# First batch's causal masks added in PSUM by TensorE, half of its q and k loaded as f16 by software DMA, and the hand-written order of all steps replaced

## The chip, the cores and the metric

The kernel runs on one core of one Trainium2 chip. The metric is the device time of one execution in microseconds (us). The engines are named as the profile names them: PE is TensorE's matmuls and PEld its weight loads, DVE is VectorE, ACT is ScalarE, POOL is GpSimd, and SP is SyncE, which here only issues DMAs. POOL issues the software DMAs (queue q0 of the profile), SP and ACT the hardware ones (q1).

## What is computed

For 8 batches of 8 heads, 576 tokens and 64 features a head, with 16 beacon keys ahead of the ordinary ones, attention is followed by a mixer over tokens and a two-layer perceptron:

```python
k_all = np.concatenate([beacon_k, k], axis=2)
v_all = np.concatenate([beacon_v, v], axis=2)
scores = scale * np.matmul(q, k_all.transpose(0, 1, 3, 2))
causal[:, Nb:] = np.triu(np.ones((S, S), dtype=bool), k=1)
scores = np.where(causal, -1000000000.0, scores)
a = softmax(scores)                # exp(scores - max) / sum
x = matmul(a, v_all)               # heads side by side: 8 x 576 x 512
u = x + (x^T @ U @ V)^T            # mixer of rank 32 over the tokens
out = u + relu(u @ w_ch1) @ w_ch2  # 512 -> 2048 -> 512
```

Inputs and outputs are f32. The kernel works in f16 with f32 sums in PSUM.

## The kernel before

**Units of work.** A "pair" is two heads of one batch, 32 pairs in all: pairs 0 to 3 are batch 0, pairs 4 to 7 batch 1, and so on. For a pair, q and k come in from HBM (`main_load` for the last 512 tokens, `head_load` for the first 64, `beacon_load` for the beacon keys). A step G (`regroup`, L251) copies the main part into a pair tile `pr`; for batch 0, whose loads arrive as f32 in `stm` and `sth`, a step H (`first_heads`, L742) also casts the head part into `hd`. A step T transposes q or k on PE (L261, L263) and copies it out of PSUM into `qT` or `kT` by DVE (L264, L265) or ACT (L109); from batch 3 on steps R let a transposing DMA do this. In the script GqV2 reads: regroup q of pair 2 by VectorE; A stands for ScalarE.

**Scores.** `score_units` (L298) makes a pair's scores in four visits, Sa to Sd, of widths 496, 464, 496 and 208 (`groups`). A visit multiplies for both heads, which sit in partitions 0 to 63 and 64 to 127 (L316, 64 rows each), and ACT takes the exponential from PSUM into one of four buffers `expt` (L321), two for each pair. Steps M (`mask_head`, L302), two a pair, then cap the masked entries on DVE: one `min` against `bigmask` over four diagonal blocks of 128 (L304) and one over the last block of 80 (L306). The caps are 65504 where a key is allowed and 0 where it isn't. Steps A (`av_unit`, L325) multiply with v (L331) and divide by the row sums on DVE (L339, L340).

**Mixer and perceptron.** X steps (`mix_units`) make `uT`: Xb.0 is `qtp` (L371), Xb.1 and Xb.2 are the `ups` products (L390, L397) and their copies by DVE and ACT. The perceptron runs in nine blocks of 512 tokens: g steps (L529, 16 a block, each four matmuls of 512 columns, ReLU by ACT and DVE), p steps (sums of operands on DVE), P steps (second layer, L620), U steps (transposing DMAs). The last three blocks make the first layer by F steps (L566).

**Order.** Nothing is scheduled at run time. `SCRIPT` (L855 on) is a list of steps, and each engine gets its instructions in the order of that list. An engine executes in order, so an instruction that waits holds all that stand behind it on its engine. Two kinds of steps do no needed work: I1 is one filler matmul of 512 columns (`keep_warm`, L239), and an ending such as ":3" on a visit puts three fillers ahead of it. A lower-case k, q, b, v or w issues a group of DMAs on POOL; for instance q1A loads q of batch 1's first four heads. Each DMA waits for the one eight places before it in its queue, whose semaphore it reuses.

**Loads of batch 0.** `load_first` (L691) puts pair 0's q on ACT's queue with the beacon keys; pair 0's k and pairs 1 to 3 are 14 DMAs on SP, all f32. v comes by POOL in halves of four heads, v0A and v0B. POOL's next loads are q1A and k1A, then w12, a quarter of the first weight matrix.

Of the kernel before, what the change touches and what calls it, by code (L numbers as in the profile page):

```python
# [9 lines left out]
F16 = mybir.dt.float16  # L10
F32 = mybir.dt.float32
# [6 lines left out]
P = 128  # L18
# [9 lines left out]
def kernel(  # L28
# [86 lines left out]
    bigmask = const.tile([P, 4, P], F16, name="bigmask", tag="bigmask")  # L115

# [181 lines left out]
    def score_units(c, qT, kT, ex):  # L298
# [11 lines left out]
        def visit(g, idle=0):  # L310
            ps = [pst([P, 512], F32, name=f"sps{i}") for i in range(2)]
            keep_warm(ps[0], idle)
            for ch, qa, w, o in groups[g]:
                for i in range(2):
                    hp = slice(D * i, D * i + D)
                    nc.tensor.matmul(  # L316
                        ps[i][:, ds(o, w)], kT[hp, c, ds(P * ch, P)], qT[hp, c, ds(qa, w)],
                        start=True, stop=True,
                    )
            for i in range(2):  # L320
                nc.scalar.activation(  # L321
                    out=ex[i][:, ds(PAD + SLOT * g, gw[g])], in_=ps[i][:, 0 : gw[g]], func=AF.Exp, scale=scale
                )
# [367 lines left out]
    def load_first():  # L691

        main = gtp.tile([P, 2, H, 4 * D], F32, name="stm", tag="gT")
        head = gtp.tile([P, 2, H, D], F32, name="sth", tag="gT")
        raw["head"] = head
        hd = [loads.tile([P, H, D], F16, name=f"hd{i}", tag=f"hd{i}") for i in range(2)]
        Ls[0] = hd, [main[:, i, :, :] for i in range(2)]

        def kload(hs):
            main_load(nc.sync, k[0], main[:, 0, hs, :], hs)  # L700
            head_load(nc.sync, k[0], head[:, 0, hs, :], hs, Nb)

        def qload(eng, hs):
            main_load(eng, q[0], main[:, 1, hs, :], hs)
            head_load(eng, q[0], head[:, 1, hs, :], hs, 0)

        qload(nc.scalar, SETS[0])
        kload(SETS[0])
        beacon_load(nc.scalar, beacon_k[0], head[:, 0, :, :], ALLH)

        nc.scalar.activation(out=warm, in_=ones, func=AF.Exp)
        for hs in SETS[1:]:
            kload(hs)
            qload(nc.sync, hs)
# [19 lines left out]
    def group(p, i, copy):  # L734
# [3 lines left out]
        regroup(Ls[b], c, i, copy, prs[p])  # L738
        if b == 0 and not any(t[0] == "H" and t[1] == "kq"[i] and t[3:] == str(p) for t in SCRIPT.split()):
            first_heads(c, i, copy)  # L740
# [21 lines left out]
    def scores_of(p):  # L762
        b, c = divmod(p, NH2)
        if p not in scs:
            scs[p] = score_units(c, qT_of(b), kTs[b % 2], ex_of(p))
# [25 lines left out]
    def step(t):  # L791
# [7 lines left out]
        elif name in "kqbv":  # L799
# [5 lines left out]
            elif name == "b":  # L805
                beacon_load(nc.gpsimd, beacon_k[b], L_of(b)[0][0], ALLH)
# [49 lines left out]
        HqA0 I1 GkA0 I1 I1 I1 GqA0 I1 I1 HkV0 u I1 I1 I1 GkV1 I1 B I1 I1 I1 TqA0 TkA0 I1 TkV1 I1 s v0A  # L856
        Sd0 Sb0 Sa0:3 I1 GqV1 TqV1 GkV2 Sc0 I1 GqV2 v0B I1 I1 Sc1 Sb1 I1 M0.0 Sd1 M0.1 TqV2 TkV2 I1 A0.0
        I1 GqV3 Sa1:2 A0.1 M1.0 Sd2 I1 GkV3 q1A M1.1 Sc2 TqA3 Sb2 I1 k1A Sa2:1 TkV3 I1 M2.0 I1 A1.0 I1
        A1.1 Sd3 Sa3:1 w12 I1 Sb3 cV M2.1 GqV4 A2.1 b1 k1B TqV4 GkA5 Sc3 I1 GkV4 I1 M3.0 q1B eA GqV5
        TkV4 I1 GkV7 TkA5 I1 w13 A2.0 Sd4 M3.1 I1 TqV5 A3.0 GkA6 b2 w10 I1 A3.1 k2 Sa4 I1 Sd5 GqV6 GqV7  # L860
        TkA7 X0.0 X0.1 Sa5:0 X0.2 Sb4 TqV7 TqV6 Sc5 TkA6 v1A g0.9 Sc4 M4.1 Sb5 M5.1 U0.0 U0.2 g0.13
        GkV11 g0.1 M5.0 g0.10 g0.0 GkV8 g0.14 q2 g0.3 g0.11 GkA9 A5.0 A5.1 Sb7 I1 w11 TkV8 GqV8 GqV9 Sa7
        g0.2 M4.0 GqV11 Sd7 Sc7 TkV11 TkA9 g0.8 A4.1 M7.0 TqA9 A4.0 p00.0 p00.1 Sb6 v1B Sa6:0 g0.12
        p00.2 TqV11 M7.1 Sc6 g0.4 Sd6 g0.15 M6.0 GkA10 w20 U0.1 M6.1 TqV8 g0.6 A7.1 A7.0 Sd9 Sc9 w21
        A6.1 g0.7 A6.0 Sd8 g0.5 Sc8 Sa8 GqV10 X1.0 v2 b3 p01.0 p01.2 X1.1 P02.0 p01.1 X1.2 W0 P01.0 Sb8
        W4 W5 W1 Sb9 Sa9 W2 U1.1 W6 P01.1 TkA10 P02.1 M8.1 M9.0 TqA10 W7 b4 M8.0 U0.3 P05.0 P05.1 q3
        P06.0 P06.1 M9.1 A8.1 A9.0 A8.0 Sa10 P03.0 P03.1 k3 g1.15 A9.1 q4 Sa11 Sd10 g1.5 g1.1 Sb10 Sc10
        g1.3 g1.2 GkV13 GqA12 M10.0 GkA12 W3 P07.0 M10.1 P07.1 GqA13 Sb11 Sd11 GqA14 Sc11 M11.1 g1.9
        M11.0 GkA14 g1.12 A10.0 g1.7 g1.10 g1.0 R12 R13 R14 g1.6 TkV12 TqV12 TkV13 P04.0 GqA16 A11.1
        g1.8 U1.0 U1.3 TqA13 GkA15 P04.1 g1.14 A11.0 k4 A10.1 Sa13 Sd12 g1.11 p10.0 g1.4 GqA17 g1.13  # L870
        Sa12 Sb12 Sc12 p11.0 GqV15 X2.0 M12.0 P11.0 GkA17 P11.1 U1.2 X2.1 GkV16 p11.1 R15 P12.0 P12.1
        R16 P16.0 TqV14 Sd13 Sb13 M12.1 p10.1 p10.2 Sc13 P16.1 b5 U2.2 M13.0 TkA14 v3 A12.1 q5 A12.0 R17
        GkA19 P15.0 P15.1 p11.2 Sa14 Sd14 Sc14 x12 P17.0 TkV15 M13.1 P13.0 U2.3 A13.0 Sb14 Z16 M14.0
        P17.1 P13.1 GqA19 GqA18 TkV16 TqA16 A13.1 g2.13 g2.10 TqV17 TqV15 M14.1 v4 g2.4 Sa15 k5 Sc15
        TkA17 P14.0 A14.0 P14.1 A14.1 Sd16 GqV20 Sb15 Sd15 M15.1 GkV18 g2.0 x14 Sc16 M15.0 g2.7 g2.5
        g2.2 A15.0 A15.1 x13 Sd17 Sb17 g2.9 U2.0 X3.0 b6 Sa16 X2.2 g2.3 x15 Sa17 Sb16 R18 R19 Z18 GkV20
        M16.1 Sc17 M17.1 M17.0 g2.1 g2.6 g2.12 M16.0 g2.8 g2.15 A17.0 U2.1 TqA19 GqA21 TqA18 X3.1 A16.1
        A17.1 g2.14 A16.0 X3.2 g2.11 p21.0 P21.0 P21.1 GqA23 GkA21 q6 TkA18 p20.0 P22.0 P22.1 TkA19 R20
        p21.1 p20.1 Sc18 Sb18 P26.0 P26.1 R21 Sc19 Sd18 Sa19 p21.2 P25.0 P25.1 GkV22 p20.2 I1 Sd19 Sa18
        M18.0 U3.0 Sb19 M19.0 P27.0 M18.1 M19.1 P23.0 GqV24 GqA22 TqV20 P27.1 x16 P23.1 g3.11 TqA21  # L880
        GkV23 TkV20 TkA21 R22 b7 A19.1 g3.7 A19.0 R23 g3.13 g3.8 g3.5 Sa21 Sb21 Sc21 P24.0 P24.1 A18.1
        A18.0 Sb20 U3.3 Sd21 Sa20 M21.1 M21.0 g3.3 g3.2 Sc20 Sd20 X4.0 g3.4 M20.0 k6 GkV24 M20.1 g3.15
        GqA26 N5 v5 TkV22 g3.12 A21.0 U3.1 A20.0 g3.10 N1 GkA26 g3.1 x17 q7 g3.0 A20.1 TqV22 TqA23 TkV23
        g3.6 g3.14 g3.9 p30.0 p30.2 A21.1 Sc23 GkV25 p31.0 Sb23 GqV25 Sa23 R24 p30.1 x18 P31.0 P31.1
        GkV27 P32.0 P32.1 TkA24 p31.1 Sc22 p31.2 U3.2 k7 Sd22 v6 Sa22 P36.0 P36.1 Sb22 x19 M22.1 Sd23
        M23.0 P35.0 R25 R26 M22.0 P35.1 X4.1 P37.0 P37.1 X4.2 GqV27 TqA24 TqA25 P33.0 U4.1 P33.1 TkA25
        P34.0 R27 g4.0 GqV28 A22.1 TkV26 GkA28 R28 M23.1 g4.11 GqV29 g4.2 g4.6 TqV26 A23.0 g4.10 A23.1
        Sd25 Sc25 A22.0 g4.4 GkV29 R29 Sb25 GkV30 Sa25 M25.0 Sd24 TqV27 P34.1 TkA27 g4.3 U4.3 TkV28
        M25.1 g4.15 g4.13 g4.9 Sc24 Sa24 x21 Sb24 M24.0 U4.2 X5.0 A25.0 M24.1 g4.8 g4.12 U4.0 GqV31 x22
        g4.1 p40.0 p40.1 GqA30 A25.1 g4.7 Sa27 Sb27 A24.1 g4.14 A24.0 g4.5 p41.0 GkV31 Sc27 x23 Sc26  # L890
        p41.2 p41.1 Sd26 P41.0 P41.1 Sa26 Sd27 M27.1 Sb26 P45.0 p40.2 P42.0 P42.1 P45.1 TkA29 x20 X5.1
        U5.3 A27.1 R30 TqV29 M27.0 P46.0 P46.1 P43.0 P43.1 g5.13 A27.0 M26.0 M26.1 Sd29 g5.11 X5.2 g5.4
        U5.1 TqV28 P47.0 g5.2 A26.1 TkA30 x27 P47.1 A26.0 N0 Sb29 Sc29 R31 N4 g5.6 N2 Sb28 Sa29 g5.0 x24
        P44.0 g5.15 TqA30 M29.1 P44.1 x25 Sd28 Sa28 v7 Sc28 M28.1 M28.0 A29.1 g5.7 g5.14 TkV31 g5.1 g5.5
        M29.0 A28.0 g5.3 N3 A28.1 Sb30 TqV31 Sa30 g5.10 A29.0 U5.0 g5.12 g5.9 x29 g5.8 N6 p51.0 p51.2
        X6.0 p50.0 Sb31 Sd30 p50.1 x26 p51.1 Sc31 P51.0 P51.1 Sd31 p50.2 Sc30 M30.0 M30.1 Sa31 M31.0 x28
        U5.2 P52.0 M31.1 P56.0 X6.1 P55.0 A31.1 V6.0 U6.1 V6.2 P56.1 A31.0 x31 P52.1 A30.1 A30.0 V6.1
        x30 P57.0 P55.1 P57.1 X6.2 X7.0 N7 P53.0 P53.1 U6.2 F61.3 X7.2 P54.0 P54.1 F62.3 F61.2 X7.1
        F66.3 F62.2 F61.0 F65.0 V6.3 F65.3 V7.0 F62.0 U7.2 F66.2 F65.1 F67.3 F63.3 F61.1 F66.0 F62.1
        F63.0 F64.3 F66.1 F65.2 F67.2 F71.3 F67.0 F75.0 F67.1 F63.1 U7.0 F71.0 V7.1 F64.0 U7.3 F63.2  # L900
        p61.0 V8.0 P61.0 V7.3 F64.2 F64.1 F76.0 F76.3 U7.1 p61.1 U6.3 p60.0 p60.1 p60.2 U6.0 P61.1 P62.0
        P62.1 P65.0 p61.2 P65.1 guard V7.2 P66.0 P66.1 P63.0 P63.1 F75.3 F72.0 F72.3 F75.2 F77.0 F73.0
        P67.0 P67.1 F73.3 F71.1 F71.2 F72.1 F72.2 F76.1 F76.2 F75.1 V8.2 V8.1 P64.0 P64.1 F77.1 F77.2
# [127 lines left out]
```

## Time and profile before

| what | us |
|---|---|
| median of 3 runs | 338.99 (338.74 to 339.47) |
| the profiled execution | 339.2 |
| its span | 337.5 |
| outside the span | 1.7 |
| PE busy | 327.8 |
| ACT busy | 228.0 |
| DVE busy | 264.8 |
| first matmul, a filler | starts at 1.59 |
| first exponential | starts at 8.89 |
| first mixer matmul (X0.0) | starts at 30.06 |
| last matmuls of the output | about 332.9 |

Times in the trace count from the start of the span. In the views, "idle" or "waits" name what ended the wait. A busy PE is not a PE at its peak, since fillers count as busy, and so does the time in which matmuls drain. A row of the timeline may merge neighbours on an engine ("x14"); the end that it shows is that of the last one's pipeline, so where PE rows follow each other, the distance of their starts is what the work took.

### The profile page before, as it was taken

How to read it: one execution, taken by the hardware profiler on the slowest of the kernel's cores; microseconds unless marked ns; L12 is line 12 of the kernel's file. 1: busy time of each engine (PE TensorE's matmuls, PEld its weight loads, DVE VectorE, ACT ScalarE, POOL GpSimd, SP SyncE). 2: the span in 40 equal slices, each digit the busy share in tenths (PEclk: the TensorE clock that was granted, in tenths of full speed). 3: DMA queues.
4: the chain of work that ended last, by engine and by line, in shares of the span. 5: the costliest groups of instructions: out<-in, count | busy, mean ns of one | idle time of the engine just before them, and what ended most of it. 6: DMA issues, size and time to landing. Idle time of an engine off the chain costs nothing.

```text
span 337.5 us, 8954 instructions
## 1 busy us (share of the span) xinstructions
PE 327.8 (97%) x3527; PEld 228.0 (68%) x3527; DVE 264.8 (78%) x690; ACT 228.0 (68%) x494; POOL 99.3 (29%) x129
## 2 busy tenths in 40 slices
PE   7989999999999999999999999999999999999994
PEld 3446466765678655766577547765688888888883
DVE  2888588985778757875888868886999999896882
ACT  4897898749778889878785799267912842644500
POOL 9765662340621602450024410000002503303300
PEclk9999999999999999999999999999999999999999
DMA  9999999999999999999979997554545501203042
GB/s 178 221 196 196 153 167 195 98 168 175 164 180 176 169 188 150 124 136 187 189 109 145 172 183 96 83 114 100 51 62 161 93 2 63 80 0 95 3 113 98
DMA packets 136145, 44.17 MB, mean 131 GB/s; under 512 B 108417, under 2 KB 131969, under 8 KB 136097
## 3 DMA queue, kind: packets, MB, share of 16 engines
q0 software_dynamic: 69008, 17.54, 61.3%
q1 hardware_dynamic: 66496, 25.66, 42.0%
q8 instruction: 29, 0.48, 0.6%
q10 hardware_dynamic: 592, 0.34, 0.3%
q14 instruction: 20, 0.16, 0.2%
HBM read 37.63 MB, written 9.44 MB: 139 GB/s over the span
## 4 chain that ended last, share of the span: by engine, by line
PE 75%; DVE 16%; DMA 3%; issue 3%; ACT 2%; SPq 0%; DVEq 0%; ACTq 0%
PE gps L529 23%; PE cpY L620 15%; PE po L331 8%; PE sps L316 8%; PE cpD L620 7%; PE cpA L620 3%; PE fpY L566 3%; DMA stm<-in_q_dram 3%; DVE gT L581 3%; DVE sT L601 2%; DVE ob L645 2%; DVE uT L404 2%; PE fpD L566 2%; PE tps L263 1%; ACT expt L321 1%
## 5 line engine op out<-in xcount | busy, mean ns | idle before, releaser
L321 ACT ACTIVATE expt<-sps 128x496 f16<-128x496 f32 (+2 forms) x256 | 111.6, 538 | 15.8 <-PE sps L316 14.3
L529 PE MATMUL gps<-uT,w 128*128 128x512 f16 x384 | 91.8, 379 | 0.0
L620 PEld LDWEIGHTS <-gT 128*128 128x128 f16 x576 | 54.6, 98 | 10.5 <-issue 2.2
L529 PEld LDWEIGHTS <-w 128*128 128x128 f16 x384 | 34.3, 98 | 37.4 <-issue 2.5
L587 POOL TENSOR_SCALAR gT<-gT 128x512 f16<-128x512 f16 x12 | 17.8, 1495 | 105.6 <-DVE gT L581 89.0
L620 PEld LDWEIGHTS <-sT 128*128 128x128 f16 x432 | 41.0, 98 | 7.8 <-issue 2.0
L331 PEld LDWEIGHTS <-expt 128*128 128x128 f16 (+1 forms) x960 | 35.5, 98 | 9.2 <-DVE expt L304 1.3
L203 POOL DMA_DIRECT2D vs<-in_v_dram x50 | 40.5, 825 | 3.2 <-DMA w<-in_moe_w_ch_dram 2.5
L539 ACT ACTIVATE gT<-gps 128x512 f16<-128x512 f32 x48 | 29.8, 630 | 15.5 <-PE gps L529 15.2
L304 DVE TENSOR_TENSOR expt<-expt,bigmask 128x512 f16<-128x512 f16 x64 | 26.7, 417 | 17.2 <-ACT expt L321 17.2
L331 PE MATMUL po<-vs,expt 128*128 128x65 f16 (+1 forms) x960 | 38.0, 194 | 1.0 <-ACT expt L321 1.0
L620 PE MATMUL cpY<-wsum,gT 128*128 128x256 f16 x288 | 36.1, 273 | 0.0
L620 PE MATMUL cpD<-w,sT 128*128 128x256 f16 x288 | 35.5, 273 | 0.3 <-DVE sT L601 0.3
L316 PE MATMUL sps<-qT,kT 64*128 64x80 f16 (+4 forms) x384 | 34.5, 282 | 0.4 <-ACT kT L109 0.3
L340 DVE TENSOR_TENSOR xb<-po,rec 128x320 f16<-128x320 f32 x64 | 31.5, 492 | 2.2
L534 DVE SCALAR_TENSOR_TENSOR gT<-gps,gT 128x256 f16<-128x256 f32 x48 | 19.8, 420 | 14.9 <-ACT gT L533 14.8
L109 ACT ACTIVATE hP<-fpY 128x512 f32<-128x512 f32 x24 | 13.7, 598 | 23.0 <-PE fpY L566 18.8
L533 ACT ACTIVATE gT<-gps 128x256 f16<-128x256 f32 x48 | 19.5, 418 | 11.5 <-PE gps L529 11.0
L316 PEld LDWEIGHTS <-kT 64*128 64x128 f16 x384 | 13.9, 94 | 18.7 <-issue 10.1
L645 DVE TENSOR_TENSOR ob<-cpY,ut 128x512 f32<-128x512 f32 (+1 forms) x28 | 18.7, 667 | 6.0 <-PE cpY L620 6.0
L566 PEld LDWEIGHTS <-wf 128*128 128x128 f16 x192 | 18.6, 98 | 3.0 <-issue 0.7
L620 PE MATMUL cpY<-w,gT 128*128 128x256 f16 x144 | 17.7, 273 | 0.0
(115 smaller groups left out, 477.6 us busy)
## 6 DMA issues: line engine op xcount, KB each, us to landing
out_dram<-ob SPq DMA_DIRECT2D x16, 512.0 KB, 4.5
st<-in_k_dram POOLq DMA_DIRECT2D x6, 512.0 KB, 8.9
st<-in_q_dram POOLq DMA_DIRECT2D x6, 512.0 KB, 8.6
vs<-in_v_dram POOLq DMA_DIRECT2D x18, 128.0 KB, 7.7
w<-in_moe_w_ch_dram POOLq DMA_DIRECT2D x4, 512.0 KB, 8.6
w<-in_moe_w_ch_dram POOLq DMA_DIRECT2D x2, 1024.0 KB, 12.6
stm<-in_k_dram SPq DMA_DIRECT2D x4, 256.0 KB, 5.0
stm<-in_q_dram SPq DMA_DIRECT2D x3, 256.0 KB, 5.6
```

The source lines that it names most:

```text
L203: nc.gpsimd.dma_start(out=dst[a : a + nq[j], j, :, :], in_=src[hs, ds(q0[j], nq[j]), :].rearrange("h p d -> p h d"))
L304: nc.vector.tensor_tensor(out=e4, in0=e4, in1=bigmask, op=ALU.min)
L316: nc.tensor.matmul(ps[i][:, ds(o, w)], kT[hp, c, ds(P * ch, P)], qT[hp, c, ds(qa, w)], start=True, stop=True,)
L321: nc.scalar.activation(out=ex[i][:, ds(PAD + SLOT * g, gw[g])], in_=ps[i][:, 0 : gw[g]], func=AF.Exp, scale=scale)
L331: nc.tensor.matmul(po[:, j, :], ex[0 : nk[c], ds(blk[(c, j)], P)], vs[0 : nk[c], ds(c * H * E + h * E, E)], start=(c == 0), stop=(c == j),)
L340: nc.vector.tensor_tensor(out=xb[:, h // 2, :, ds(D * (h % 2), D)], in0=po[:, :, 0:D], in1=r.broadcast_to([P, NT, D]), op=ALU.mult)
L529: nc.tensor.matmul(g, w1[:, cc, ts(dc, P)], uT[:, cc, ds(ring(t0), 512)], start=(cc == 0), stop=(cc == NCC - 1))
L534: nc.vector.scalar_tensor_tensor(out=gT[:, dc, H2:512], in0=g[:, H2:512], scalar=0.0, in1=gT[:, dc, 0:H2], op0=ALU.max, op1=ALU.subtract,)
L539: nc.scalar.activation(out=gT[:, dc, :], in_=g, func=AF.Relu)
L566: nc.tensor.matmul(ps[:, i, :], a[:, kk, ts(2 * mp + i, P)], b[:, kk, :], start=opens and i == 0 and kk == 0, stop=kk == 1, skip_group_che ...
L620: nc.tensor.matmul(ps[:, i, :], a[:, f, ds(P * i, P)], b[:, f, :], start=opens and i == 0 and f == 0, stop=f == NK - 1, skip_group_check=True,
L645: nc.vector.tensor_tensor(out=out, in0=ps[:, ii, :], in1=other, op=ALU.add)
```

## The change

**Masks.** For batch 0 (`masked = b == 0`) the DVE steps M0.0 to M3.1 are gone from the script. `fill_masks` builds two small tiles at the start on DVE, `sel` (65504 on a diagonal) and `nm` (0 where a key is allowed, -65504 where it isn't). After each diagonal block of scores, four matmuls (two column halves for two heads, 64 rows each, as the scores) add sel x nm to the scores in PSUM, ahead of the exponential. That makes 20 matmuls a pair and 80 in all. The other batches keep the mask on DVE.

**Loads.** SP and ACT load pairs 0 and 1 alone as f32. k, q and beacon keys of pairs 2 and 3 come by POOL's software DMA straight to f16 tiles (steps k0B, q0B, b0B), as in later batches, so these two pairs need no H step.

**Order.** Every line of the script is different. It has 37 I1 steps and 7 fillers on visits, as before. For batch 1 and later the set of steps is the same, apart from which of DVE and ACT makes some G and T steps.

```diff
+    def fill_masks():
+        nc.vector.memset(sel, 0.0)
+        nc.vector.memset(nm[:, 1, 0:HP], -F16_MAX)
+        nc.vector.memset(nm[:, 0, HP:P], 0.0)
+        for i in range(2):
+            r = slice(HP * i, HP * i + HP)
+            for h in range(2):
+                nc.vector.tensor_scalar(
+                    out=sel[r, h, ds(HP * h, HP)], in0=ident[r, r], scalar1=F16_MAX, scalar2=None, op0=ALU.mult
+                )
+                nc.vector.tensor_scalar(
+                    out=nm[r, h, ds(HP * h, HP)], in0=mask[r, r], scalar1=F16_MAX, scalar2=None, op0=ALU.subtract
+                )
...
-                        start=True, stop=True,
+                        start=True, stop=not masked, skip_group_check=masked,
                     )
+                if masked and qa == q0[ch]:
+                    a = Nb if ch == 0 else 0
+                    for h, e in ((0, HP), (1, min(P, w))):
+                        for i in range(2):
+                            hp = slice(D * i, D * i + D)
+                            nc.tensor.matmul(
+                                ps[i][:, ds(o, e - a)], sel[hp, h, :], nm[hp, h, a:e],
+                                start=False, stop=True, skip_group_check=True,
+                            )
...
-        HqA0 I1 GkA0 I1 I1 I1 GqA0 I1 I1 HkV0 u I1 I1 I1 GkV1 I1 B I1 I1 I1 TqA0 TkA0 I1 TkV1 I1 s v0A
+        I1 I1 HkA0 I1 I1 I1 u I1 I1 I1 I1 HqV0 I1 I1 I1 I1 I1 I1 I1 I1 GqV0 GkV0 I1 I1 I1 v0A TqV0 GkA1
+        TkA0 I1 TkA1 I1 Sb0 Sd0 GqV1 TqV1 Sc0 Sc1 Sa1:2 Sb1 I1 k0B GkV2 q0B cV Sa0:3 GqA2 GkV3 I1 Sd1 I1
...
```

Three places show what moves. The first is the head of POOL's queue, from the last DMA of v0A on (`vs` is v; `st` and `hd` are the main and head parts of k and q; `w` is the first weight matrix). Before:

```order
L203 DMA vs_126<-in_v_dram 80x4x64
L193 DMA vs_126<-in_beacon_v_dram 16x4x64
L203 DMA vs_126<-in_v_dram 112x4x64
L203 DMA vs_126<-in_v_dram 128x4x64 x3
L203 DMA vs_126<-in_v_dram 80x4x64
L196 DMA st_429<-in_q_dram 128x4x256
L190 DMA hd_427<-in_q_dram 80x4x64
L196 DMA st_428<-in_k_dram 128x4x256
L190 DMA hd_426<-in_k_dram 64x4x64
L180 DMA w_108<-in_moe_w_ch_dram 128x4x512
```

And after the change, where `st_144`, `st_145`, `hd_142` and `hd_143` are batch 0's second half, `st_464` and `st_465` batch 1's first:

```order
L222 DMA vs_127<-in_v_dram 80x4x64
L215 DMA st_144<-in_k_dram 128x4x256
L209 DMA hd_142<-in_k_dram 64x4x64
L215 DMA st_145<-in_q_dram 128x4x256
L209 DMA hd_143<-in_q_dram 80x4x64
L212 DMA hd_142<-in_beacon_k_dram 16x4x64
L215 DMA st_465<-in_q_dram 128x4x256
L209 DMA hd_463<-in_q_dram 80x4x64
L215 DMA st_464<-in_k_dram 128x4x256
L209 DMA hd_462<-in_k_dram 64x4x64
L199 DMA w_109<-in_moe_w_ch_dram 128x4x512
L212 DMA vs_127<-in_beacon_v_dram 16x4x64
```

Five DMAs stand ahead of q1A and k1A, and v0B has moved from ahead of them to behind w10. The second place is ACT's queue between the exponentials of batch 0's first two pairs (`expt` written from `sps`) and its last. Before, from pair 2's visits on:

```order
L321 ACTIVATE expt_121<-sps_435 128x496
L109 ACTIVATE qT<-tps 128x64
L109 ACTIVATE qT<-tps 128x512
L321 ACTIVATE expt_120<-sps_452 128x464
L321 ACTIVATE expt_121<-sps_453 128x464
L321 ACTIVATE expt_120<-sps_462 128x496
L321 ACTIVATE expt_121<-sps_463 128x496
```

And after the change, from pair 1's last visit to pair 3's first:

```order
L349 ACTIVATE expt_123<-sps_386 128x208
L349 ACTIVATE expt_124<-sps_387 128x208
L109 ACTIVATE pr<-st_145 128x512
L109 ACTIVATE kT_125<-tps 128x80
L109 ACTIVATE kT_125<-tps 128x512
L109 ACTIVATE qT<-tps 128x64
L109 ACTIVATE qT<-tps 128x512
L109 ACTIVATE qT<-tps 128x64
L109 ACTIVATE qT<-tps 128x512
L109 ACTIVATE pr<-st_464 128x512
L349 ACTIVATE expt_123<-sps_519 128x496
L349 ACTIVATE expt_124<-sps_520 128x496
```

Copies of pairs 2 and 3 now stand on ACT, and the last of them, `pr<-st_464` (GkA5), needs k1A's data. The third place is PE's queue at the first visit of scores. Before, with fillers behind two visits:

```order
L316 MATMUL sps_258<-qT,kT_124 128x208
L316 LDWEIGHTS kT_124
L316 MATMUL sps_259<-qT,kT_124 128x208
L316 LDWEIGHTS kT_124
L316 MATMUL sps_264<-qT,kT_124 128x464
L316 LDWEIGHTS kT_124
L316 MATMUL sps_265<-qT,kT_124 128x464
L241 LDWEIGHTS ident
L241 MATMUL sps_270<-ident 128x512
```

And after the change, in which `msk` holds sel and nm:

```order
L335 MATMUL sps_269<-qT,kT_125 128x464
L335 LDWEIGHTS kT_125
L335 MATMUL sps_270<-qT,kT_125 128x464
L344 LDWEIGHTS msk
L344 MATMUL sps_269<-msk 128x64
L344 LDWEIGHTS msk
L344 MATMUL sps_270<-msk 128x64
L344 LDWEIGHTS msk
L344 MATMUL sps_269<-msk 128x128
L344 LDWEIGHTS msk
L344 MATMUL sps_270<-msk 128x128
```

The four mask matmuls follow the scores of their block within the same visit. Over the whole of PE's queue, matmuls of the full array (shapes 128\*128 and 80\*128 in the profile) alternate with those of a part of it (64\*128, 32\*128, 128\*32: scores, masks and parts of the mixer). Such changes number 179 in the order before, of which 36 lie ahead of X0.0, and 150 in the changed order, of which 20 lie ahead of X0.0. Ahead of X0.0 stand 42 of the 44 fillers before, and 39 after.

## The prediction on record

> **What bounds the kernel now.** I read the page's totals first, then PE's longest wait behind the start, then the busy time by stretches.
>
> ```profile
> span 337.5 us, 8954 instructions
> PE 327.8 (97%) x3527; PEld 228.0 (68%) x3527; DVE 264.8 (78%) x690; ACT 228.0 (68%) x494; POOL 99.3 (29%) x129
> ```
> ```profile
> PE fpD L566 <- DVE ob L645: 0.5, 1, 0.5
> ```
> ```profile
> 34.20:260.00 225.80, 225.76 (x2523) 148.21 (x2521) 178.53 (x482) 170.28 (x372) 57.53 (x75) 1.00 1.27 143
> 260.00:333.00 73.00, 71.99 (x652) 63.22 (x649) 61.37 (x108) 31.35 (x59) 17.31 (x12) 1.00 0.24 66
> ```
>
> The columns of a stretch are its length, then PE, PEld, DVE, ACT and POOL with their counts. PE is busy 225.76 of 225.80 us from 34.2 to 260 and lacks 1.0 us up to 333, of which the wait above is half. Nothing that shortens a wait of another engine can help there; only less work on PE can. What is left is the start, where PE's busy time is partly filler:
>
> ```profile
> L241 PE MATMUL idle<-ident 128*128 128x512 f16 x35 | 12.5, 440 | 1.6 <-POOL ident masks.py:199 1.6
> L241 PE MATMUL sps<-ident 128*128 128x512 f16 x7 | 2.2, 381 | 0.0
> ```
>
> That is 42 fillers in the first 36 us. So the question is when X0.0, the first mixer matmul, can start, and how much PE work lies behind it. The timeline of the start (PE's and ACT's rows):
>
> ```profile
> 1.59 4.68 PE L241 MATMUL idle<-ident 128*128 128x512 f16 x13 [1.59 <-POOL ident masks.py:199]
> 6.11 0.20 PE L261 MATMUL tps<-ident,hd 80*128 80x80 f16 x1
> 8.89 5.71 ACT L321 ACTIVATE expt<-sps 128x208 f16<-128x208 f32 x14 [0.35 <-PE sps L316]
> 15.46 2.53 ACT L321 ACTIVATE expt<-sps 128x496 f16<-128x496 f32 x6 [0.86 <-PE sps L316]
> 17.88 0.72 ACT L109 ACTIVATE qT<-tps 128x64 f16<-128x64 f16 x2
> 18.46 4.72 ACT L321 ACTIVATE expt<-sps 128x464 f16<-128x464 f32 x10
> 23.04 0.65 ACT L109 ACTIVATE pr<-st 128x512 f16<-128x512 f16 x1
> 24.00 1.06 ACT L321 ACTIVATE expt<-sps 128x496 f16<-128x496 f32 x2 [0.31 <-PE sps L316]
> 30.06 0.59 PE L371 MATMUL qtp<-xb,Usb 128*32 128x128 f16 x20
> ```
>
> ACT makes batch 0's 32 exponentials (14+6+10+2) almost without a gap from 8.89 to 25.06: **ACT sets the pace of the start**, and X0.0 follows at 30.06, 5.0 us after the last exponential.
>
> **From the start to X0.0, after the change.** I walk along ACT's queue, since it is the full one.
>
> First, PE's 20 fillers ahead of the first transposes instead of 13. Thirteen lasted from 1.59 to about 6.1; seven more at the later pace of 0.22 us (a g matmul of the same 512 columns, 0.86/4 below) put the first transposes at 7.6 instead of 6.11. Then the transposes of q and k of pair 0, a group of five matmuls each:
>
> ```profile
> 13.09 0.21 PE L261 MATMUL tps<-ident,hd 80*128 80x80 f16 x1 [0.28 <-DVE hd L743]
> 13.36 0.20 PE L261 MATMUL tps<-ident,hd 80*128 80x80 f16 x1
> ```
>
> From one group's start to the next's is 0.27. Then ACT's copies of kT for pair 0 and pair 1 (0.6 each by the row at 17.88; before, DVE made pair 1's). The first exponential starts at about 9.5 instead of 8.89, a loss of 0.6.
>
> From there 32 exponentials at 5.71/14 = 0.41 us take 13.1 us. Six copies stand among them in the new order (GqA2, GqA3, TkA3, TqA3, TqA2, GkA5), at about 0.55 us (0.58 from 17.88 to 18.46; 0.65 for `pr`, whose end overlaps the next) 3.3 us. Before there were two. That ends at 25.9, if no data is late; I take 26.0. The last exponential is thus 0.9 us later.
>
> Behind it, before: masks and divisions on DVE, which the queue of DVE delayed.
>
> ```profile
> L304 DVE TENSOR_TENSOR expt<-expt,bigmask 128x512 f16<-128x512 f16 x8 | 3.3, 413 | 0.4 <-ACT expt L321 0.4
> L306 DVE TENSOR_TENSOR expt<-expt,mask 80x80 f16<-80x80 f16 x8 | 1.5, 188 | 0.0
> 27.68 0.41 DVE L304 TENSOR_TENSOR expt<-expt,bigmask 128x512 f16<-128x512 f16 x1
> 28.30 0.62 PE L331 MATMUL po<-vs,expt 128*128 128x65 f16 x15
> ```
>
> Pair 3's last exponential ended at 25.06, but its second mask ran at 27.68, since it stood behind copies, and its product with v at 28.30. After the change this chain is gone: all 16 DVE instructions (3.3 + 1.5 us). Behind the last exponential PE does A3.1 (about 0.5), a filler (0.22), A3.0 (0.5), three groups of transposes (0.8) and the two small products of step eA with their changes of shape (an estimate, 0.4): 2.4 us, so X0.0 starts at **28.4**, a gain of **1.7 us**. DVE divides A3.0 at about 28.3, so it just keeps up; that is what is late next.
>
> **The mask matmuls** fall ahead of X0.0, all 80. No row shows them. The nearest are scores of 80 columns, which go in pairs side by side, and products with v of 65 columns:
>
> ```profile
> 23.58 0.39 PE L316 MATMUL sps<-qT,kT 64*128 64x336 f16 x6
> 23.90 0.60 PE L241 MATMUL idle<-ident 128*128 128x512 f16 x2
> 22.76 0.65 PE po L331 x15
> ```
>
> Six matmuls of 336, 80 and 80 columns for two heads take 0.32 us with one change of array shape; 15 products with v take 0.65, 0.04 each at most. A block's four mask matmuls have about 190 columns a head: 0.08 us side by side, 0.16 one after another; 20 blocks make 1.6 to 3.2 us. I take 1.6, as the scores' pairs do, and count none of it on the path: a visit with masks takes PE some 0.4 us while ACT needs 0.8 for its two exponentials, and fillers stand around it. If that cover were gone it would cost the 1.6 to 3.2. `fill_masks` adds 11 small DVE instructions at the start. DVE waited there:
>
> ```profile
> 5.85 0.22 DVE L743 CAST hd<-sth 80x128 f16<-80x128 f32 x1 [4.20 <-DMA sth<-in_beacon_k_dram]
> ```
>
> Even at that row's 0.22 each they are 2.4 us inside a wait of 4.20: nothing.
>
> **The loads** decide whether ACT stands still at GqA2 or GkA5.
>
> ```profile
> stm<-in_k_dram SPq DMA_DIRECT2D x4, 256.0 KB, 5.0
> st<-in_k_dram POOLq DMA_DIRECT2D x2, 256.0 KB, 7.6
> vs<-in_v_dram POOLq DMA_DIRECT2D x8, 64.0 KB, 6.7
> 8.90:15.40 6.50, 6.22 (x65) 3.01 (x64) 5.61 (x22) 5.71 (x14) 5.35 (x8) 1.00 1.64 222
> 12.97 0.75 POOL L196 DMA_DIRECT2D st<-in_k_dram  x1
> 3.04 3.62 POOL L203 DMA_DIRECT2D vs<-in_v_dram  x5
> 7.13 3.63 POOL L203 DMA_DIRECT2D vs<-in_v_dram  x5
> ```
>
> Two heads as f32 land as 256 KB, four as f16 land as the same 256 KB: the main parts of batch 0's second half shrink from 1024 to 512 KB. At 222 GB/s, the stretch's rate (its last column), that is 2.3 us less. v0B (three parts of 64 KB and two smaller, some 290 KB, 1.3 us) moves behind q1A, k1A and w10. k1A's main part was issued at 12.97 and landed 7.6 later, near 20.6; now 20.6 - 2.3 - 1.3 = **17.0**, if a transfer is paid by the bytes that land. If it isn't, the five DMAs of pairs 2 and 3 take the place of v0B and k1A stays at 20.6; I take 17.0, as the rate held over f32 and f16 together, and keep 20.6 as the other end. k0B takes v0B's place, behind v0A's issues, at 3.04 + 3.62 = 6.7, and lands 5.0 to 7.6 later, by 14.3; q0B, two issues on, by 15.7. ACT reaches GqA2 at about 15.4 and GkA5 at 18.7. Both are on time, GqA2 barely. SP loses eight DMAs; behind them only the small loads of U and V waited, which come earlier.
>
> The Trainium skill's page "SBUF — State Buffer" (section "SBUF: two separate sides") has a rule against this part: while DVE copies in a mode that takes the port it shares with GpSimd, descriptors of a POOL DMA cannot be written. By that rule the loads would come later, not earlier (the last rival). Here five issues of v took POOL 3.62 us from 3.04, while DVE rested, and 3.63 from 7.13, while it copied, so the trace does not show it.
>
> **Behind X0.0** PE is full, so I count its work. A change of array shape has a price:
>
> ```profile
> 43.99 0.97 PE gps L529 x4
> ...
> 55.27 0.86 PE gps L529 x4
> 28.86 0.38 PE L316 MATMUL sps<-qT,kT 64*128 64x496 f16 x2
> 29.17 0.39 PE L241 MATMUL idle<-ident 128*128 128x512 f16 x1
> ```
>
> Four g matmuls take 0.86 us ahead of full-array work and 0.97 ahead of scores; two score matmuls of 496 columns take 0.31, where 496 of g's 512 columns (0.86/4) would be 0.21. So each change costs 0.10 us, entering or leaving. Behind X0.0 the order had 179 - 36 = 143 of them and has 150 - 20 = 130: 13 fewer, **-1.3 us**. Fillers behind X0.0 go from 2 to 5, 3 x 0.22 = **+0.65**. Work that stood ahead of X0.0 and is now behind it: TkA7 (0.27) and the visits Sd4, Sa4, Sd5 (208, 496 and 208 columns: 0.09 + 0.21 + 0.09 without the changes): **+0.65**. Sum: 0.0. ACT still has those visits' six exponentials to make (at most 2.5 us) when g begins, so I add **+0.2** for PE waits; from nothing to 1.0.
>
> Sum: -1.7 + 0.0 + 0.2 = -1.5. From the profiled execution, 339.2, that is **337.7 us**; this execution stands 0.2 above the median of the runs, 338.99.
>
> **Rivals.**
> - *k1A is late, and ACT stands at GkA5* with the exponentials of pairs 2 and 3 behind it. For: five DMAs now stand ahead of it in one queue where each waits for the one eight places before; against: the bytes. Every us that it lands past 18.7 moves X0.0 by one. At 20.4 the gain is gone; at 22, 1.4 later than before, the time is 337.7 + 3.3 = **341.0, slower**. Chance 0.14.
> - *Each mask matmul waits for the one before it*, like a change of shape, 0.10: 0.4 us a visit and block on top. ACT's 0.8 a visit still covers most; the four narrow visits, with about half of that, and the first one don't, some 5 x 0.25 = 1.25: **339.0**, the same. Chance 0.08. Below nothing it can't be, since matmuls are only added.
> - *The late blocks lose it*: DVE's sums already hold PE there (the 0.5 at L566 above), and the new order hits two or three such waits more, 1.5 us: **339.2**, the same. Chance 0.10.
> - *The extra fillers are hidden in waits, and DVE's relief is worth more*: the three behind X0.0 cost nothing (-0.65) and data is early enough that A3 follows at once (-0.7): **336.3**. Chance 0.20.
> - *POOL's issues are held by DVE's copies*, of which one takes 0.68 us:
>
> ```profile
> L265 DVE COPY qT<-tps 128x512 f16<-128x512 f16 x6 | 4.1, 680 | 0.0
> ```
>
> Five added issues held by one copy each make 3.4 us, so that k1A lands at 20.4 and X0.0 moves by 1.7: **339.4**, the same. The two rows of v's issues speak against it. Chance 0.03. By the figure on the Trainium skill's page "SBUF — State Buffer" (about 3.1 us for an overlapped issue instead of 0.62) my estimate would be five times 2.5, some 12 us instead of 3.4.
>
> **How the numbers follow.** My forecast has 0.45. Faster by over 0.2% (about 0.7 us, what a measurement here can tell from no change) takes 0.45, 0.20 and 0.04 from the edges of the three cases that are the same, in all 0.69; these three keep 0.16; slower has the late loads and 0.01 of them, 0.15. The forecast's own range is 336.6 to 338.6, from X0.0 at 27.7 to 29.2. For 8 in 10 I go from 335.6, below the good rival, to 340.4, which leaves out the worst of the late loads.
>
> **What would show it.** X0.0 at 28.4 (27.7 to 29.2), the first exponential at 9.5, the last one of batch 0 at 26.0, ACT without a wait at GkA5 (`pr<-st`), PE rows of four g still 0.86 or 0.97, and a distance from X0.0 to the end of the span that stays at 307.5. It would be wrong if ACT's list shows a DMA wait of over 1 us before 26, or if PE waits behind 60 us.

## The result: slower, and the profile after

The changed kernel takes 351.27 us (median of 4 runs, 349.66 to 352.88) against 338.87 us of the kernel before beside it: ratio 1.0364, 95 % interval 1.0309 to 1.0418. That is 12.4 us more, where the prediction had 1.3 us less than the median shown. Two executions further down, one each of `f1_later` and `f3_later`, were over 1.5 % slower than the fastest of their kernel and are left out of the numbers for these two. The profiled execution took 350.51 us; its page has these totals:

```profile
span 348.9 us, 9096 instructions
PE 333.8 (96%) x3607; PEld 231.4 (66%) x3607; DVE 253.1 (73%) x664; ACT 236.3 (68%) x511; POOL 102.4 (29%) x134
```

PE's share of 96 % instead of 97 looks harmless. The stretches show where the span went (after; columns as in the prediction: length, PE, PEld, DVE, ACT, POOL, granted clock, DMA share, GB/s):

```profile
34.20:60.00 25.80, 25.80 (x321) 14.67 (x319) 18.83 (x62) 23.83 (x62) 13.32 (x18) 1.00 1.72 175
60.00:200.00 140.00, 132.50 (x1393) 86.17 (x1391) 95.88 (x260) 105.12 (x223) 37.99 (x50) 0.98 1.30 140
200.00:260.00 60.00, 60.00 (x672) 38.11 (x669) 46.83 (x127) 47.69 (x102) 4.72 (x6) 1.00 0.83 118
```

The same stretch of the kernel before:

```profile
60.00:200.00 140.00, 139.96 (x1534) 92.14 (x1533) 106.15 (x284) 112.45 (x241) 42.99 (x56) 1.00 1.49 159
```

From 60 to 200 us PE now stands 7.5 us, where it stood 0.04, and its clock is 0.98 on average. From 34.2 to 60 and from 200 to 260 it is full in both.

A finer account counts, between the starts of neighbouring matmuls, what exceeds the columns of the first at the pace of the g matmuls (512 in 0.216 us) and the prediction's 0.10 for a change of shape, where it is over 0.04. It is my own sum over the matmuls' rows; fillers count as work in it, a half clock as loss:

| lost by PE, us | 0 to 30 | 30 to 60 | 60 to 100 | 100 to 110 | 110 to 200 | 200 to end | all | span less all |
|---|---|---|---|---|---|---|---|---|
| before | 4.9 | 0.2 | 0.0 | 0.0 | 0.1 | 1.7 | 6.9 | 330.7 |
| after | 4.8 | 1.0 | 2.5 | 5.5 | 4.2 | 0.5 | 18.5 | 330.4 |

By this account PE's work is the same to 0.3 us. **The loss is PE waiting, or at half clock behind a wait, between 60 and 200 us**: 12.1 us more there, 0.8 more from 30 to 60, 1.2 less at the end. Ahead of 30 us, where the new masks and loads stand, nothing is lost.

What it waits for, the chain of the changed kernel says (start, length, what):

```profile
84.49 7.47 DMA raw<-pr
92.06 0.24 ACT pr L109
...
95.82 5.74 DMA raw<-pr
...
101.65 0.63 ACT pr L109
```

A step R is a transposing DMA from a pair tile `pr` to a tile `raw`. The pair tiles have three buffers (`pairs = ctx.enter_context(tc.tile_pool(name="pairs", bufs=3))`), so a regroup G may only fill a tile when the transpose that still reads it has landed. ACT's timeline around the largest loss, then PE's (start, length, engine, line, what; in brackets the idle time before and what ended it):

```profile
95.41 1.61 ACT L567 ACTIVATE gT<-gps 128x512 f16<-128x512 f32 x3
101.65 0.63 ACT L109 ACTIVATE pr<-st 128x512 f16<-128x512 f16 x1 [4.63 <-DMA raw<-pr]
102.19 1.45 ACT L349 ACTIVATE expt<-sps 128x464 f16<-128x464 f32 x4
```
```profile
98.71 1.05 PE L648 MATMUL cpA<-w,gT 128*128 128x256 f16 x8
102.78 1.59 PE L418 MATMUL ups<-ident,xb 128*128 128x112 f16 x16 [3.02 <-ACT expt L349]
104.74 3.33 PE L648 MATMUL cpY<-w,gT 128*128 128x256 f16 x16
```

The `pr` row is GqA19. In the new script it stands one step behind R15 (`g1.14 R15 GqA19 Sb12`), whose tile it refills; in the script before, GkA19 comes 22 steps behind R15. R15's DMA was issued at 95.82 and landed at 101.56. ACT stood 4.63 us, pair 12's exponentials stood behind it, and PE, which needed their PSUM tiles back, stood 3.02 us. The last row is the half clock: 16 matmuls of 256 columns in 3.3 us, which take 1.8 elsewhere.

The view of `raw` sums up who waited, first after, then before:

```profile
  ACT pr L109: 7.6, 2
  DVE qT L310: 4.1, 1
  DVE pr L272: 3.6, 2
  ACT kT L109: 2.6, 2
...
  ACT qT L109: 0.6, 1
...
DMA to landing us min/median/max: 3.1/7.1/12.4
```
```profile
  ACT pr L109: 1.5, 1
  DVE kT L291: 1.0, 1
...
DMA to landing us min/median/max: 3.1/4.6/10.8
```

ACT and DVE stand 18.5 us for transposes, in the kernel before 2.5 (besides POOL's gates, which are meant to wait; an exponential's wait of 2.0 us that the view lists too came behind copies out of `raw` and isn't counted). 11.2 of the 18.5 are `pr`, regroups that wait for a buffer; the rest are copies that read `raw` too soon.

### The profile page after: what moved, and what is told of

The parts are those of the page before. It is cut to its first block, busy times and chain, and to the rows that moved or that the text cites. A ratio compares the mean times of both kernels' runs of the same rounds, so it can differ in the third digit from the quotient of the medians.

```text
span 348.9 us, 9096 instructions
## 1 busy us (share of the span) xinstructions
PE 333.8 (96%) x3607; PEld 231.4 (66%) x3607; DVE 253.1 (73%) x664; ACT 236.3 (68%) x511; POOL 102.4 (29%) x134
## 4 chain that ended last, share of the span: by engine, by line
PE 76%; DMA 8%; ACT 7%; issue 3%; DVE 3%; POOL 1%; SPq 0%; ACTq 0%; DVEq 0%; POOLq 0%
PE gps L557 17%; PE cpY L648 16%; PE cpD L648 8%; DMA raw<-pr 8%; PE po L359 8%; PE sps L335 6%; PE fpY L594 6%; ACT expt L349 4%; PE cpA L648 4%; PE fpD L594 3%; PE idle L260 3%; PE tps L282 1%; PE fpA L594 1%; PE ups L425 1%; PE ups L418 1%
## 5 line engine op out<-in xcount | busy, mean ns | idle before, releaser
L335 PE MATMUL sps<-qT,kT 64*128 64x80 f16 (+4 forms) x384 | 36.4, 281 | 1.3 <-DVE xb L368 0.4
L368 DVE TENSOR_TENSOR xb<-po,rec 128x320 f16<-128x320 f32 x64 | 31.5, 492 | 2.2
L109 ACT ACTIVATE hP<-fpY 128x512 f32<-128x512 f32 x24 | 13.7, 598 | 26.1 <-PE fpY L594 12.5
L323 DVE TENSOR_TENSOR expt<-expt,bigmask 128x512 f16<-128x512 f16 x56 | 23.3, 417 | 9.5 <-ACT expt L349 9.5
L335 PEld LDWEIGHTS <-kT 64*128 64x128 f16 x384 | 15.0, 94 | 19.5 <-issue 11.6
L109 ACT ACTIVATE kT<-raw 128x512 f16<-128x512 f16 x17 | 19.2, 1130 | 2.6 <-DMA raw<-pr 2.6
## 6 DMA issues: line engine op xcount, KB each, us to landing
w<-in_moe_w_ch_dram POOLq DMA_DIRECT2D x2, 1024.0 KB, 11.3
```

The source lines that it names most:

```text
L109: nc.scalar.activation(out=out, in_=in_, func=AF.Copy)
L323: nc.vector.tensor_tensor(out=e4, in0=e4, in1=bigmask, op=ALU.min)
L335: nc.tensor.matmul(ps[i][:, ds(o, w)], kT[hp, c, ds(P * ch, P)], qT[hp, c, ds(qa, w)], start=True, stop=not masked, skip_group_check=masked,)
L368: nc.vector.tensor_tensor(out=xb[:, h // 2, :, ds(D * (h % 2), D)], in0=po[:, :, 0:D], in1=r.broadcast_to([P, NT, D]), op=ALU.mult)
```

## The experiments

The theory: **the new order puts G steps and copies too close behind the transposes they depend on**, and ACT and DVE, which work in order, carry the wait to PE. Rivals: the new parts shift every later batch by one staging buffer and so make things late in any order; or the transposes themselves are late, and whatever comes next waits.

**The two halves of the order.** Two kernels join the scripts at X1.0. `h1_start` is the changed kernel up to there and the old order behind, `h2_rest` the reverse, with the old masks and loads.

```diff
-SCRIPT = one of the two orders
+SCRIPT = first order up to X1.0, then the other order without the steps already done
```

> The changed kernel's new parts and its order up to the mixer's first matmul of batch 1 (step X1.0, at 57.2 us in its trace), and behind it all steps in the order of the kernel before. If the loss lies in the changed order behind 60 us alone, the 1.0 us that the change is ahead at X1.0 stays: 338.9 - 1.0 = 337.9, between 337 and 339.5. If it comes of the new parts (batch 0's pairs 2 and 3 now take a turn of the staging buffers, so that every later batch uses the other buffer), the rest is late in any order: 348 to 352.

> The other half: the kernel before, its masks and loads untouched, with its own order up to X1.0 and behind it all steps in the changed order. If the order behind 60 us is the cause: 351.3 + 1.0 = 352.3, between 349 and 354. If the new parts are: 338 to 340.

Measured: `h1_start` 341.32 us (10 runs) against 339.21, ratio 1.0053 [1.0036, 1.0069]; `h2_rest` 352.11 us, ratio 1.0357 [1.0299, 1.0415]. The loss goes with the order behind X1.0 and needs neither new masks nor new loads. But `h1_start` missed its range: no gain of 1.0, a loss of 2.1. The 1.0 us was itself work put off: at X1.0 the changed order still has TkV11, TqV11 and the visits Sd9, Sc9, Sd8 and Sa8 to do and, of PE's needed work, is ahead by Sb9 alone; that is about 0.9 us of PE at the prediction's prices (an estimate). And in its trace PE loses 1.2 us at the joint, at 58 to 61.4 us, and waits for a v load at 42:

```profile
42.38 0.65 PE L359 MATMUL po<-vs,expt 80*128 80x65 f16 x16 [0.49 <-DMA vs<-in_v_dram]
```

**The waits.** `f1_later` moves five steps of the changed order: the regroups GqA16, GqA19 and GkV21 and the copies TqA23 and TqV22.

```diff
-g1.14 R15 GqA19 Sb12
+g1.14 R15 Sb12
...
+GqA19 TqA15
```

> The changed kernel with five steps moved a little later, at which ScalarE or VectorE stood and waited for a transposing DMA to land: the regroups of q of pairs 16 and 19 and of k of pair 21 (each fills the buffer that such a DMA still reads), and the reordering copies of q of pairs 22 and 23. If those waits cost the time, TensorE's losses of 0.75 us at 93, 3.2 us at 102.8, 2.0 us at half clock behind it and 1.3 us at 143 go, and part of the 2 us around 180: 341 to 345. If the waits stand beside the cause only (the transposes are late in any case and something else waits for them next): 348 to 352.

Measured: 345.06 us (342.27 to 345.57, three runs), ratio 1.013 [1.0062, 1.0198]: 6.2 us less than the changed kernel, at the upper edge of the theory's range. The losses at 93, 103 and 143 and the half clock are gone. PE's wait for DVE's sums, 1.07 us at 187 in the changed kernel, stands at 181 and has grown to 3.61. DVE's row, then PE's:

```profile
179.51 0.30 DVE L272 COPY pr<-st 128x512 f16<-128x512 f16 x1 [3.71 <-DMA raw<-pr]
```
```profile
181.07 1.05 PE L648 MATMUL cpY<-wsum,sT 128*128 128x256 f16 x8 [3.61 <-DVE sT L629]
```

The row of DVE is GqV26, which waits for R24; sums that PE needs stand behind it. R24, issued 7.5 us earlier than in the changed kernel, took 4.8 us to land instead of 3.3. `f2_later` moves it too:

> The changed kernel with the five steps moved later and a sixth, the regroup of q of pair 26 on VectorE, which in the run with five stood 3.7 us for the transpose of pair 24 while TensorE waited 3.8 us for the sums behind it. If this wait is a cause of its own: 345.3 - 3.7 = 341.6, between 340.5 and 343. If time lost there only shows what the other queues lack anyway: 344 to 346.

Measured: 348.21 us (345.81 to 349.06), 3.2 us slower than with five steps moved. Both ranges, with the theory and against it, missed. GqV26 no longer waits, but the next of its kind does, GqA28 on ACT, four steps behind R25:

```profile
187.35 0.63 ACT L109 ACTIVATE pr<-st 128x512 f16<-128x512 f16 x1 [3.90 <-DMA raw<-pr]
```
```profile
188.50 0.89 PE L359 MATMUL po<-vs,expt 128*128 128x65 f16 x15 [2.74 <-ACT expt L349]
```

R25, issued 2.3 us earlier than in `f1_later`, took 8.3 us to land instead of 3.3. This trace is of the fastest of five executions; what the other four lose beyond it isn't shown. `f3_later` moves GqA28 down to GkA28:

> The changed kernel with six steps moved as before and a seventh: the regroup of q of pair 28 on ScalarE, which in the run with six stood 3.9 us for the transpose of pair 25, while TensorE waited 2.9 us for the exponentials behind it and then had half clock for 3.4 us. If this was the next wait of the same kind: 348.2 - 2.9 - 1.4 = 343.9, between 342 and 345.5. If the waits only move on: 346.5 to 349.

Measured: 341.78 us (341.28 to 344.52, four runs), ratio 1.008 [1.0028, 1.0132], 0.2 below the theory's range. So the waits are of one kind, but repairing them one by one uncovers the next.

**Nearly all buffer waits at once.** `a4_buffers` leaves the changed order as it is and gives the pair tiles a fourth buffer; `b4_buffers` does the same to the kernel before. In both the room comes from two small tiles that now lie in buffers of other pools.

```diff
-    pairs = ctx.enter_context(tc.tile_pool(name="pairs", bufs=3))
+    pairs = ctx.enter_context(tc.tile_pool(name="pairs", bufs=4))
```

> The changed kernel, its order untouched, with a fourth buffer for the regrouped pairs (the room comes from two small tiles of the guard and of the general branch that are laid into other pools). No regroup then has to wait for the transpose of three pairs before it. If those waits are the cause, the losses at 93, 102.8 with the half clock behind it, 143 and most of that at 180 to 187 go, about 8 us, and only the copies that read a transpose too soon stay: 343, between 341 and 346. If the transposes themselves are late and whatever comes next waits for them: 348 to 352.

> The kernel before with the same fourth buffer. Its engines wait 2.5 us in all for these transposes and TensorE none of it: 338.5 to 339.5 by the theory of the waits. If the fourth buffer brought something of its own (other addresses, later guard), it would show here: under 338 or over 340.

Measured: `a4_buffers` 343.10 us (342.21 to 344.63) against 339.45, ratio 1.0114 [1.0076, 1.0151]; `b4_buffers` 339.12 us, ratio 1.0001 [0.9985, 1.0017]. **With the order untouched the fourth buffer takes away 8.2 of the 12.4 us, as forecast (343)**, and it brings nothing in the kernel before, where regroups hardly wait. (Each against its own measurement of the kernel before, it takes away 8.7.) The regroups' waits fall from 11.2 to 1.5 us. The transposes land no earlier for it (median 7.6 us), so late transposes alone aren't the cause; why they land later in the changed order than in the old one (4.6) isn't shown. GqA19 again, and the stretch:

```profile
96.33 0.60 ACT L567 ACTIVATE gT<-gps 128x512 f16<-128x512 f32 x1 [1.18 <-PE gps L557]
96.83 0.62 ACT L109 ACTIVATE pr<-st 128x512 f16<-128x512 f16 x1
97.34 1.46 ACT L349 ACTIVATE expt<-sps 128x464 f16<-128x464 f32 x4
```
```profile
60.00:200.00 140.00, 138.63 (x1494) 90.60 (x1493) 100.70 (x272) 112.11 (x239) 42.08 (x56) 1.00 1.32 149
```
```profile
DMA to landing us min/median/max: 3.1/7.6/11.4
```

PE lacks 1.4 us in the stretch instead of 7.5. What stays, about 4 us, is many waits of 0.1 to 0.4 us from 47 to 200 us, among them copies that read `raw` too soon (DVE stands 6.2 us for it, ACT 5.8), less the 1.2 us by which PE waits less behind 200; in this execution a start that is 0.9 us later than the changed kernel's adds to it (X0.0 at 29.70; the next section says why).

**The same wait in the old order.** `r1_sooner` moves GqA19 right behind R15 in the kernel before.

```diff
-R15 P12.0
+R15 GqA19 P12.0
```

> The kernel before with one step moved: the regroup of q of pair 19 on ScalarE, right behind the transpose of pair 15 whose buffer it fills, as the changed order has it. ScalarE would stand from 96.5 us to that transpose's landing at 102.3 us. If such a wait of 5 us is enough by itself, TensorE runs dry for 2 to 4 us and runs at half clock after it: 342 to 346. If ScalarE has the slack: 338.5 to 340.

Measured: 340.28 us, ratio 1.0026 [1.0004, 1.0047], so 1.1 us: just above the range for slack, well below the theory's. In the traced execution (341.23) ACT waits about as long as in the changed kernel, PE much less. ACT's row of the kernel before, then ACT's and PE's of this one:

```profile
101.27 2.43 ACT L321 ACTIVATE expt<-sps 128x208 f16<-128x208 f32 x6 [2.06 <-PE sps L316]
```
```profile
102.99 0.63 ACT L109 ACTIVATE pr<-st 128x512 f16<-128x512 f16 x1 [3.89 <-DMA raw<-pr]
```
```profile
103.91 0.62 PE L331 MATMUL po<-vs,expt 128*128 128x65 f16 x15 [0.93 <-ACT expt L321]
106.94 0.78 PE L316 MATMUL sps<-qT,kT 64*128 64x496 f16 x10 [0.67 <-ACT kT L109]
```

ACT had 2.06 us of idle time there anyway, and PE has matmuls in its queue that need nothing from ACT. The wait's length alone doesn't set its price: 4.63 us of ACT cost PE 3.02 us and the half clock in one order, 3.89 us cost it 0.93 and 0.67 in the other.

**The new parts alone.** In the old order: `m1_masks` has the masks in PSUM, `l1_loads` the f16 loads (k0B, q0B, b0B behind v0A), `p1_parts` both.

```diff
-            scs[p] = score_units(c, qT_of(b), kTs[b % 2], ex_of(p))
+            scs[p] = score_units(c, qT_of(b), kTs[b % 2], ex_of(p), b == 0)
```
```diff
-TkV1 I1 s v0A Sd0
+TkV1 I1 s v0A k0B q0B b0B Sd0
```

> The kernel before in its own order, with one part of the change alone: batch 0's masks are added by TensorE in PSUM, and VectorE's eight masking steps of that batch are gone. If the start is paced by ScalarE's exponentials, 1.6 us of mask matmuls lie beside them and the shorter way from exponentials to attention gains little: 338.3 to 339.5 (the kernel before: 339.0). If the mask matmuls stand in TensorE's row and hold up the scores behind them: 339.7 to 341.

> The kernel before in its own order, with the other part alone: q and k of batch 0's last two pairs are loaded by software DMA on GpSimd's queue as f16, right behind the first v load, and batch 0's masks stay on VectorE. If the f32 loads on the hardware queues were not what the start waited for: 338.5 to 339.7. If the later turn of the staging buffers (every later batch takes the other buffer) makes later loads or transposes late in any order: 341 to 350.

> Both parts of the change in the order of the kernel before, without the changed order of the start. If the parts are harmless and only the order behind 60 us costs: 338 to 339.8. If they cost together what the start-with-old-rest kernel lost (341.3): 340.8 to 342, and then that kernel's 2 us are not its seam's.

Measured against 339.18: masks 339.22, ratio 0.9997 [0.9984, 1.0009]; loads 340.01, ratio 1.0024 [1.0010, 1.0039]; both 339.98, ratio 1.0023 [1.0005, 1.0042]. **In this order the masks change nothing, and the loads cost 0.8 us** (0.3 over the range for harmless loads). ACT's first exponentials of pair 1 to 2 and PE's wait ahead of them:

```profile
16.56 2.53 ACT L330 ACTIVATE expt<-sps 128x496 f16<-128x496 f32 x6 [1.68 <-PE sps L316]
```
```profile
PE tps L261 <- DMA hd<-in_q_dram: 1.0, 1, 1.0
```

q0B's head part lands 1.0 us too late for pair 2's transposes; ACT idles 1.68 us there, where it idled 0.86. By the rival of the shifted staging buffers `l1_loads` would have taken 341 to 350 us; it did not.

**Does the changed start gain at all?** `s1_start` joins the scripts at X0.0 instead of X1.0.

> The changed kernel's parts and its order up to X0.0, the first mixer's first matmul (28.8 us in its trace, 30.06 in that of the kernel before), and behind it all steps in the order of the kernel before, the ones that this order already has ahead of X0.0 coming first. By the prediction on record the start is worth 1.5 us: 337.5. If X0.0 comes earlier only because work is put off behind it (TensorE loses 4.8 us ahead of 30 us in the changed kernel and 4.9 us in the kernel before), nothing is won: 338.8 to 341.

Measured: 343.56 us (341.94 to 345.29), ratio 1.0144 [1.0100, 1.0188], slower than both ranges. The joint is to blame: steps that the old order has ahead of X0.0 now come at once behind it, and a load that they read isn't there:

```profile
31.48 0.22 PE L280 MATMUL tps<-ident,hd 80*128 80x80 f16 x1 [1.64 <-DMA hd<-in_k_dram]
```

PE loses 3.2 us from 30 to 40, 0.15 in the kernel before; part of it is half clock, from 31.5 to 35.0. The trace is of the fastest of four executions (341.94). So this run can't settle it; the next section goes by the traces.

**The end.** Behind 200 us the changed order loses 0.5 us of PE, the old one 1.7. `v1_tail` joins the old order with the changed one at X6.0, `v2_tail` at P54.1.

> The kernel before up to X6.0 (about 240 us), its masks and loads untouched, and behind that the changed order. Behind 250 us TensorE waits 0.50, 0.64, 0.17 and 0.26 us in the kernel before and 0.29 us in the changed one. If that is the order's doing: 339.2 - 1.2 = 338.0, between 337.4 and 338.6. If the joint makes waits of its own or the late waits come in any order: 339 to 340.

> The kernel before with the changed order only behind P54.1 (about 260 us), where the two orders have done the same steps but for three, so that the joint should cost nothing; the joint at X6.0 cost 1.2 us between 241 and 243 us. If the changed order behind it keeps its 0.29 us of waits against 1.57 us: 339.4 - 1.2 = 338.2, between 337.6 and 338.8. If not: 339.2 to 340.

Measured: 339.60 us, ratio 1.0007 [0.9993, 1.0021], and 339.19 us, ratio 0.9996 [0.9982, 1.0011]. Neither shows the gain (338.0 and 338.2). The waits at 276, 283 and 324 us are gone, but `v1_tail` loses 1.2 us at its joint (241 to 243) and `v2_tail` 1.0 at 261:

```profile
261.30 0.93 PE L566 MATMUL fpY<-tc,wf 128*128 128x256 f16 x7 [0.85 <-ACT hP L109]
```

No version here beats the kernel before.

## Why the prediction was wrong, point by point

**The start was read rightly.** These rows of the changed kernel answer those of before:

```profile
1.59 6.29 PE L260 MATMUL idle<-ident 128*128 128x512 f16 x20 [1.59 <-POOL ident masks.py:199]
7.72 0.20 PE L280 MATMUL tps<-ident,hd 80*128 80x80 f16 x1
...
9.43 0.25 PE L344 MATMUL sps<-msk 64*128 64x64 f16 x4
9.52 0.25 PE L335 MATMUL sps<-qT,kT 64*128 64x208 f16 x2
...
28.82 0.46 PE L399 MATMUL qtp<-xb,Usb 128*32 128x128 f16 x20
```
```profile
9.71 6.19 ACT L349 ACTIVATE expt<-sps 128x464 f16<-128x464 f32 x14
...
19.06 0.68 ACT L109 ACTIVATE pr<-st 128x512 f16<-128x512 f16 x1
19.70 1.59 ACT L349 ACTIVATE expt<-sps 128x496 f16<-128x496 f32 x4
21.50 5.24 ACT L349 ACTIVATE expt<-sps 128x496 f16<-128x496 f32 x12 [0.21 <-PE sps L344]
```

- First transposes at 7.72 (forecast 7.6), first exponential 9.71 (9.5), last one of batch 0 done at 26.7 (26.0), X0.0 at 28.82 (28.4, within 27.7 to 29.2).
- A block's four mask matmuls take 0.09 us (9.43 to 9.52; forecast 0.08), hidden; `m1_masks` confirms nothing gained or lost.
- GqA2 "on time, barely" did not follow from the prediction's own bounds (q0B by 15.7, ACT there at 15.4), but it was on time.
- GkA5 (19.06) has no wait: the main parts landed at 12.1 for k0B (forecast by 14.3), 13.7 for q0B (by 15.7) and 17.6 for k1A (17.0). The rival of late loads fell in this order, as did the ones of mask matmuls and of POOL's issues.

**The 1.2 us by which X0.0 came earlier were not a gain.** From X0.0 to the end of the span, less PE's losses there, work of 306.4 us is left after (348.86 - 28.82 - 13.66) and 305.5 before (337.54 - 30.06 - 1.95). So 0.9 us of work had only been put off; the prediction's terms behind X0.0 (-1.3, +0.65, +0.65) sum to 0.0. The start is worth some 0.4 us (1.24 - 0.85) instead of 1.5, in this pair of executions. Others would have given another number: the first fillers come 0.43 us apart instead of 0.22, and how many do changes from trace to trace, 8 in the kernel before and 9 in the changed one. In the seven traces with the new start X0.0 moves with that count, from 28.31 us (6 slow fillers, `s1_start`) to 29.70 (13, `a4_buffers`), as 20 fillers instead of 13 stand ahead of the first transposes there. In the six with the old start untouched it stays between 29.58 and 30.08 (6 to 12). So what the start is worth on average stays open.

**The step that failed is the term "+0.2 for PE waits; from nothing to 1.0".** It measured +11.7: 13.66 us of losses behind X0.0 against 1.95; with the 0.4 of the start that is the 11.3 us between the two profiled executions. The reasoning was "Behind X0.0 PE is full, so I count its work". PE is full there because in the old order ACT and DVE wait only 2.5 us for transposes and almost none of it reaches PE; that is a property of the order that the change replaces, not of the kernel. Behind X0.0 I compared only counts (changes of shape, fillers, moved work), not how far each step stands behind the transpose that it depends on. What the waits are made of is shown: regroups for a buffer, 8.2 us (`a4_buffers`). The rest, about 4 us, is not fully settled: the loads' 0.8 us is from another order, and the copies that read too soon are seen waiting, but they were not changed alone.

**The rival "the late blocks lose it"** named the right kind of trouble, new waits in the new order, in the wrong place (behind 260 us the new order lost less) and eight times too small. The prediction did name the signs that it had failed: PE's waits behind 60 us, and a distance from X0.0 to the end that does not stay at 307.5 (it is 320.0).

## What to carry to other kernels

When a whole order is replaced, a queue that was full is no evidence that it stays full: list each step that waits on a DMA or on a buffer that a DMA still reads, and compare its distance behind the issue, in microseconds of work on its engine, with the longest landing in the trace (here up to 10.8 us before), not with the shortest. Or give the buffer one more copy, which here repaired most of the order without touching it. What a wait costs depends on what PE still has to do, so look at what is queued behind the waiting instruction and what PE has beside it. And a milestone that comes earlier counts only after the work put off behind it has been taken away, and after it has been seen in more than one execution.

## What the runs showed of the hardware

**The half clock followed a wait, but not by its length.** Granted clock by stretches, first in the changed kernel (around PE's wait of 3.02 us), then in `f2_later` (2.74 us), then in `f1_later` (3.61 us):

```profile
97.40:100.80 3.40, 1.96 (x30) 1.18 (x30) 2.28 (x6) 0.00 (x0) 0.49 (x1) 1.00 1.14 158
100.80:104.30 3.50, 1.52 (x17) 1.38 (x17) 0.00 (x0) 2.65 (x6) 0.00 (x0) 0.51 1.62 127
104.30:107.70 3.40, 3.40 (x21) 2.20 (x20) 1.62 (x3) 3.40 (x7) 0.00 (x0) 0.50 0.46 57
```
```profile
188.60:192.10 3.50, 3.50 (x22) 1.64 (x21) 2.40 (x7) 1.90 (x3) 0.00 (x0) 0.51 2.58 129
```
```profile
175.90:179.30 3.40, 1.56 (x18) 0.93 (x14) 0.00 (x0) 2.86 (x6) 0.00 (x0) 1.00 1.16 127
179.30:182.80 3.50, 1.73 (x17) 1.14 (x18) 3.29 (x8) 1.55 (x3) 0.00 (x0) 1.00 0.53 106
```

The stretches follow the trace's own changes of clock, which lie whole multiples of 3.413 us apart (in the changed kernel 5.27, 100.84 and 107.67: 28 and 2 of them). A wait of 2.74 us brought 3.4 us of half clock and one of 3.02 us brought 6.8, in which PE lost some 2 us more (5.5 from 100 to 110 less the wait's 3.2); the longest, 3.61 us, brought none. In `s1_start` waits of 0.50 and 1.64 us close together brought 3.4 us of it, from 31.54 to 34.96. The Trainium skill's page "TensorE: Matmul & The Clock Gate" (section "Why this matters for your kernels") advises against idle gaps of over about 3 us, and its section "What's actually happening" has the activity watched in free-running windows of 3413 ns. The lengths of the half clock (one and two such windows) agree with the windows; by the gap's length alone the trace disagrees. What PE's activity in a window must fall below stays open: busy 1.96 of 3.40 us was followed by half clock, 1.56 was not (draining matmuls count as busy here).

**A transposing DMA of the same size took 3.1 to 12.4 us to land.** The slowest, R22 and R23 (12.4 and 11.1 us, issued at 158.8 and 163.6), ran beside eight loads that POOL issued from 157.7 to 164.0, with a DMA share of 2.0 and 2.3 while they were under way; those that landed in 3.1 to 3.3 us had one of 0.5 to 1.0. That the loads make them slow was not tried by itself.
